# Second projection of block 2 as seven products of quarters, with the order of all steps rewritten from block 1 on

## The chip, the cores and the metric

The kernel runs on one core of one Trainium2 chip. The metric is the device time of one execution in microseconds (us), as a median over runs. The engines are TensorE (PE in the profile; its weight loads are PEld), VectorE (DVE), ScalarE (ACT), GpSimd (POOL) and SyncE (SP), whose queue issues most DMAs.

## What is computed

The reference runs a retention layer over q, k and v (8 sequences, 8 heads, 576 positions, 64 per head) and feeds its output, 4608 tokens of 512, to two projections with a sine between them:

```python
scores = scale * np.matmul(q, k.transpose(0, 1, 3, 2))
Dmat = np.where(rel >= 0, gamma[:, None, None] ** rel, 0.0)      # rel = i - j
x = np.matmul(scores * Dmat, v)        # -> [4608 tokens, 512]
h = x @ w_in                           # 512 -> 2048
s = np.sin(alpha * h)
g = h + s * s / (alpha + 1e-09)
out = g @ w_out                        # 2048 -> 512
```

Inputs and output are float32; the kernel multiplies in float16 and sums in float32.

## The kernel before, in words

**Blocks.** The tokens are nine blocks of 512. Blocks 0 to 7 are the first 512 positions of each sequence; block 8 holds the last 64 positions of all eight (the "last tokens", class `Ends`, whose input tile is `xS`).

**Retention.** For each sequence, q and k are loaded by SP (`load`, L1345 to L1357), scaled and cast to float16 (`cast`, L1396, mostly on GpSimd), and transposed by a DMA on SP's queue (`crossed`, L1418). TensorE then computes outer sums of k and v (`outer`, L1506), scores (`scores`, L1564), values (`values`, L1606) and the part from earlier positions (`add_states`, L1628). All of these are 64x64 matmuls, four of them side by side in the array. VectorE masks the scores (`masked`, L1576), GpSimd carries the state (`more`, L1551 and L1552; `to_state`, L1544), and `keep` copies the result from PSUM to the block's input tile `xT` (L1320 on ScalarE, L1322 on VectorE).

**First projection and sine.** Of each block the 2048 features are 16 chunks of 128. `project` (L1745) is four matmuls of 512 columns into a PSUM bank. `sine` (L1753, ScalarE) reads the bank; `square` is on ScalarE (L1762), VectorE or GpSimd (both L1764); `product` (L1769, VectorE) adds the square, scaled, to the bank's value and writes `gT`. The bank is free after the product. Six banks are passed around (`op`, `h0` to `h2`, `m0`, `m1`), and the retention matmuls and the second projection use the same six.

**Second projection, two ways.** In blocks 0 to 2, `gemm2` (L1785) multiplies directly: 64 matmuls of 512 columns per block, and four `finish` steps copy the result and store it. In blocks 3 to 8 the product of `gT` (2 by 2 quarters) and `w_out` (2 by 2 quarters) is made by Winograd's scheme from seven products of quarters: `part_product` (L1849) is 16 matmuls of 256 columns, so 112 per block. For that VectorE makes eight sums of quarters of `gT` per block (`row_sum`, L1832, each 128x1024, float16, both inputs in SBUF), and once for all blocks eight sums of quarters of `w_out` (`weight_sum`, L1822). `after_product` adds the seven results up: five adds on VectorE (L1880, L1882, L1895) and two copies on ScalarE (L1878, L1893). S3 and T1 are written in place, over `gT` and `w_out`.

**The order.** `TABLE`, a text of some 1,200 lines, lists every step in the order in which it is issued, with its engine (V, A, G), its PSUM bank and the SBUF tile that it takes (`@`). Each engine and queue runs its steps in that order; semaphores do the rest. So the table decides what waits behind what. A line reads, for example:

```
project 2 7 h2
square 2 7 A @ss3
row_sum 3 S3 1 V
part_product 3 1 op
```

The first is chunk 7 of block 2 into bank `h2`; then its square on ScalarE into tile `ss3`; a sum of `gT`'s quarters of block 3 on VectorE; the first of block 3's seven products.

Of the kernel before, what the change touches and what calls it, by code (L numbers as in the profile page):

```python
# [9 lines left out]
F32 = mybir.dt.float32  # L10
F16 = mybir.dt.float16
# [379 lines left out]
gemm2 1 0 h2
product 2 2
gemm2 1 8 h0
gemm2 1 9 h0
gemm2 1 10 h0
sine 2 3 @s1
sine 2 6 @s0
square 2 1 A @ss1
product 2 1
at.scores 3 1 1 m0  # L400
square 2 6 A @ss0
sine 2 0 @s3
square 2 0 A @ss3
at.to_state 3 0 A
product 2 6
at.scores 3 1 0 m1
gemm2 1 11 h0
product 2 0
project 2 4 h1
gemm2 1 1 h2  # L410
sine 2 4 @s2
square 2 4 A @ss2
square 2 3 V @ss1
at.masked 3 1 1 @ret1
project 2 9 m0
gemm2 1 2 h2
product 2 3
product 2 4
project 2 13 h1
gemm2 1 3 h2  # L420
at.masked 3 1 0 @ret3
finish 1 2 V
sine 2 9 @s0
square 2 9 A @ss0
product 2 9
sine 2 13 @s3
finish 1 0
at.scores 3 0 1 m1
at.masked 3 0 1 @ret0
cast 4 k 1 G @k162  # L430
at.outer 4 (0,1) op h0
square 2 13 G @ss3
at.evict_bank 4 0 A @kvs0
at.scores 3 0 0 m0
at.masked 3 0 0 @ret2
project 2 14 h2
at.evict_bank 4 1 V
product 2 13
at.to_state 4 0 A @s160
at.more 4 1 @s321  # L440
project 2 8 op
at.values 3 1 False m1
at.values 3 0 False m0
at.values 3 0 True
at.values 3 1 True
at.add_states 3 0
at.add_states 3 1
sine 2 8 @s2
sine 2 14 @s1
square 2 14 V @ss1  # L450
at.more 4 2 @s320
at.keep 3 0 A V @xT0
at.keep 3 1 A
product 2 14
project 2 10 h0
project 2 11 h1
project 2 12 m0
sine 2 10 @s0
square 2 10 G @ss2
square 2 8 A @ss0  # L460
sine 2 11 @s3
at.to_state 4 1 G
product 2 10
product 2 8
square 2 11 G @ss3
product 2 11
sine 2 12 @s1
project 2 15 m1
sine 2 15 @s0
project 2 5 h2  # L470
sine 2 5 @s2
square 2 5 A @ss1
product 2 5
square 2 15 G @ss2
product 2 15
crossed 4 0 k @kT1
crossed 4 1 q @qT1
load 5 k 1 @raw1
at.more 4 3 @s321
crossed 4 0 q @qT0  # L480
square 2 12 A @ss0
product 2 12
load 5 k 0 @raw4
at.to_state 4 3 G
wait_for_w_out 3
load 5 v 0 @raw0
at.to_state 4 2 A
crossed 4 1 k @kT0
load 5 q 1 @raw2
load 0 v 2  # L490
load 1 v 2
make_mask_halved
project 3 0 h0
sine 3 0 @s3
square 3 0 A @ss2
weight_sum T3 0 V
product 3 0
gemm2 2 0 op
cast 5 v 0 G @v162
cast 5 k 1 G @k160  # L500
load 0 k 2
load 1 k 2
cast 5 q 1 G @q161
project 3 1 h1
sine 3 1 @s2
project 3 2 h2
sine 3 2 @s0
gemm2 2 1 op
project 3 3 m0
sine 3 3 @s1  # L510
square 3 2 A @ss3
load 5 v 1 @raw0
gemm2 2 2 op
gemm2 2 3 op
load 5 q 0 @raw1
project 3 4 m1
cast 5 k 0 G @k163
product 3 2
square 3 3 A @ss2
product 3 3  # L520
finish 2 0
sine 3 4 @s3
square 3 4 A @ss2
project 3 6 h0
sine 3 6 @s3
at.scores 4 0 0 m0
at.masked 4 0 0 @ret3
product 3 4
gemm2 2 4 op
gemm2 2 5 op  # L530
square 3 1 A @ss1
product 3 1
cast 5 v 1 G @v163
square 3 6 A @ss0
gemm2 2 6 op
project 3 7 h1
at.scores 4 1 0 m1
sine 3 7 @s1
product 3 6
cast 0 v 2 G  # L540
at.masked 4 1 0 @ret1
square 3 7 A @ss1
at.scores 4 1 1 m0
at.masked 4 1 1 @ret0
product 3 7
project 3 5 h2
gemm2 2 7 op
sine 3 5 @s3
square 3 5 A @ss2
product 3 5  # L550
project 3 9 h0
weight_sum T2 0 V
load 0 q 2
project 3 10 m0
finish 2 1
project 3 11 h2
# [680 lines left out]
def kernel(  # L1237
# [18 lines left out]
    nc = tc.nc  # L1256
# [772 lines left out]
```

## Time and profile before

| | before |
|---|---|
| runs shown | 297.47 us median (296.52, 297.47, 299.5) |
| profiled execution | 297.29 us |
| its span, first to last instruction | 295.6 us |
| busy: PE, PEld, DVE, ACT, POOL | 96%, 62%, 76%, 74%, 48% |
| granted TensorE clock | 1.00 of full throughout |
| HBM read and written | 36.75 MB, 9.44 MB |

The span leaves out what lies around the first and last instruction, here 1.7 us. Durations in the profile are of single instructions; in a group's row, the busy time is the union, and the mean is over the instructions. A PE instruction's end is modelled, so its length says little: the distance from one start to the next says how fast TensorE works. The profile's chain of waits, followed back from the last instruction, lists merged pieces by their distance in time. In the timeline the pieces of one engine may overlap by the length of the last instruction.

### The profile page before, as it was taken

Reading aid. Unit: us, or ns where it says so; the run is one execution under the profiler, and the core shown is the slowest. Engines: PE = TensorE matmul, PEld = TensorE weight load, DVE = VectorE, ACT = ScalarE, POOL = GpSimd, SP = SyncE. Lnnn points to the kernel's source line nnn. Section 1 sums busy time; section 2 is a strip of 40 time slices with the busy share of each in tenths; the row PEclk is TensorE's granted clock in tenths of the full one; section 3 lists DMA queues with packets and bytes.
Section 4 is the critical chain, followed back from the end, with each engine's and each line's share of the span. In section 5 each row is a group of like instructions: output and inputs, shape, how many; then the busy total and the mean of one; then the engine's idle time right before and its main releaser. Section 6 shows DMA issues by size and latency. Waiting matters only on the chain.

```text
span 295.6 us, 8403 instructions
## 1 busy us (share of the span) xinstructions
PE 284.6 (96%) x3480; PEld 182.2 (62%) x3480; DVE 225.0 (76%) x316; ACT 218.2 (74%) x361; POOL 141.0 (48%) x151
## 2 busy tenths in 40 slices
PE   6799999999999999999999999999999999999993
PEld 4565545555545544456667666666776677676883
DVE  2596979788358677899987898969868785877863
ACT  2578945997695997977878886698689869888500
POOL 5693687664798676636349935756232000000000
PEclk9999999999999999999999999999999999999999
DMA  7999999999997989969899996965323101200124
GB/s 219 347 234 210 253 294 311 262 270 260 226 197 185 163 160 239 226 154 208 156 237 158 256 181 157 243 121 128 87 81 98 38 2 38 73 20 17 57 71 123
DMA packets 121766, 49.95 MB, mean 169 GB/s; under 512 B 78720, under 2 KB 119680, under 8 KB 121728
## 3 DMA queue, kind: packets, MB, share of 16 engines
q1 hardware_dynamic: 118208, 45.04, 63.6%
q0 software_dynamic: 2688, 4.19, 7.8%
q8 instruction: 27, 0.44, 0.7%
q10 hardware_dynamic: 832, 0.18, 0.4%
q14 instruction: 11, 0.09, 0.1%
HBM read 36.75 MB, written 9.44 MB: 156 GB/s over the span
## 4 chain that ended last, share of the span: by engine, by line
PE 85%; DMA 6%; DVE 3%; ACT 2%; POOL 1%; SPq 1%; issue 0%; ACTq 0%; POOLq 0%
PE hps L1745 39%; PE hps L1849 23%; PE ops L1785 14%; DMA w_in<-in_moe_w_in_dram 4%; PE o L1606 3%; PE sc L1564 2%; DMA raw<-in_k_dram 2%; DVE S L1832 1%; PE kv L1506 1%; DVE gT L1769 1%; SPq L1350 1%; PE o L1628 1%; ACT ss L1762 1%; POOL k L1396 1%; ACT s L1753 1%
## 5 line engine op out<-in xcount | busy, mean ns | idle before, releaser
L1769 DVE SCALAR_TENSOR_TENSOR gT<-ss,inva,hps 128x512 f16<-128x512 f16 x144 | 103.5, 743 | 36.4 <-ACT ss L1762 33.1
L1745 PE MATMUL hps<-xT,w_in 128*128 128x512 f16 (+1 forms) x532 | 120.4, 372 | 0.5 <-DMA w_in<-in_moe_w_in_dram 0.4
L1753 ACT ACTIVATE s<-hps,alpha_t 128x512 f16<-128x512 f32 x144 | 96.0, 682 | 31.0 <-PE hps L1745 30.2
L1745 PEld LDWEIGHTS <-w_in 128*128 128x128 f16 x596 | 65.8, 114 | 51.4 <-DMA w_in<-in_moe_w_in_dram 0.9
L1762 ACT ACTIVATE ss<-s 128x512 f16<-128x512 f16 x125 | 76.9, 629 | 6.1 <-DVE gT L1769 3.5
L1785 PE MATMUL ops<-w_out,gT 128*128 128x512 f16 x192 | 46.0, 380 | 0.0
L1849 PEld LDWEIGHTS <-gT 128*128 128x128 f16 x384 | 37.3, 98 | 7.6
L1396 POOL TENSOR_TENSOR k<-raw,cn 128x1024 f16<-128x1024 f32 (+1 forms) x17 | 29.8, 1755 | 17.8 <-DMA raw<-in_k_dram 15.1
L1849 PEld LDWEIGHTS <-S 128*128 128x128 f16 x288 | 28.0, 98 | 6.5 <-DVE S L1832 0.5
L1785 PEld LDWEIGHTS <-gT 128*128 128x128 f16 x192 | 17.8, 98 | 20.4
L1396 POOL TENSOR_TENSOR q<-raw,cn 128x1024 f16<-128x1024 f32 x13 | 25.1, 1937 | 4.3 <-PE o L1606 3.5
L1849 PE MATMUL hps<-w_out,S 128*128 128x256 f16 x192 | 22.9, 273 | 0.2 <-DVE S L1832 0.2
L1849 PE MATMUL hps<-T,gT 128*128 128x256 f16 x192 | 22.8, 273 | 0.0
L1849 PE MATMUL hps<-w_out,gT 128*128 128x256 f16 x192 | 22.8, 273 | 0.0
L1551 POOL TENSOR_TENSOR s<-kvs,cn 128x256 f32<-128x256 f32 x21 | 13.8, 658 | 16.5 <-ACT kvs L1320 8.8
L1322 POOL CAST v<-raw 128x1024 f16<-128x1024 f32 x10 | 10.7, 1074 | 20.6 <-DMA raw<-in_v_dram 17.9
L1576 DVE TENSOR_TENSOR ret<-sc,mask 128x1024 f16<-128x1024 f32 x16 | 19.1, 1219 | 1.6 <-PE sc L1564 1.6
L1832 DVE TENSOR_TENSOR S<-gT,S 128x1024 f16<-128x1024 f16 x24 | 18.7, 786 | 0.1
L1552 POOL TENSOR_TENSOR kvs<-s,kvs 128x256 f32<-128x256 f32 x21 | 16.8, 802 | 3.6 <-DVE kvs L1322 1.2
L1320 ACT CAST xT<-o 128x1024 f16<-128x1024 f32 (+1 forms) x15 | 16.3, 1125 | 2.4 <-PE o L1628 2.2
L1576 DVE TENSOR_TENSOR ret<-sc,mask_halved 128x768 f16<-128x768 f32 x16 | 15.1, 953 | 3.4 <-PE sc L1564 3.2
L1745 PE MATMUL hps<-xS,w_in 128*128 128x512 f16 x64 | 14.8, 379 | 0.0
(78 smaller groups left out, 264.8 us busy)
## 6 DMA issues: line engine op xcount, KB each, us to landing
raw<-in_q_dram SPq DMA_DIRECT2D x16, 512.0 KB, 5.6
out_dram<-osb SPq DMA_DIRECT2D x32, 256.0 KB, 2.3
raw<-in_k_dram SPq DMA_DIRECT2D x8, 512.0 KB, 6.1
raw<-in_v_dram SPq DMA_DIRECT2D x8, 512.0 KB, 6.1
raw<-in_v_dram SPq DMA_DIRECT2D x32, 128.0 KB, 3.6
raw<-in_k_dram SPq DMA_DIRECT2D x32, 128.0 KB, 3.1
w_in<-in_moe_w_in_dram POOLq DMA_DIRECT2D x4, 512.0 KB, 11.7
w_out<-in_moe_w_out_dram POOLq DMA_DIRECT2D x4, 512.0 KB, 12.7
```

Of the source, the lines that this page charges most:

```text
L1320: eng.copy(d_, s_)
L1396: eng.tensor_tensor(dst[:, a0:a1].rearrange("p a r t d -> p t (a r) d"), t_.rearrange("p (t a) x -> p t a x", t=2)[:, :, a0:a1].rearrange( ...
L1551: nc.gpsimd.tensor_tensor(s32, self.kvs[:, c - 1], g1.unsqueeze(2).to_broadcast([P, 4, D]), MULT)
L1552: nc.gpsimd.tensor_tensor(self.kvs[:, c], s32, self.kvs[:, c], ADD)
L1576: nc.vector.tensor_tensor(ret.rearrange("p t (z x) -> p (t z) x", z=2)[:, :, 0:n], sc.rearrange("p t (z x) -> p (t z) x", z=2)[:, :, 0:n], ...
L1745: matmul(hps_of[n, fc][0][:, cols], w_in16[fc // 4][:, a, fc % 4 :: 4], xs[n][:, a, cols], start=(a == 0 and part != 1), stop=(a == KT - 1 ...
L1753: nc.scalar.activation(s_t, hps, mybir.ActivationFunctionType.Sin, bias=0.0, scale=alpha_t[:, fc : fc + 1],)
L1762: nc.scalar.activation(ss_t, s_t, mybir.ActivationFunctionType.Square)
L1769: nc.vector.scalar_tensor_tensor(gT[n][:, fc, :], ss_t, inva[:, fc : fc + 1], hps, MULT, ADD)
L1785: matmul(ops[n, c, cols.start][:, cols], gT[n][:, fk, c * P : (c + 1) * P], w_out16[:, fk, cols], start=(fk == 0), stop=(fk == FC - 1), sk ...
L1832: made = eng.tensor_tensor(out_, x, y, op)
L1849: matmul(acc[:, 256 * j : 256 * j + 256], lhs[:, x, 128 * j : 128 * j + 128], rhs[:, x], start=(tag is not None and j == js[0] and p == 0 ...
```

## The change

1. Block 2's second projection becomes seven products too: its 16 `gemm2` steps and four `finish` steps go, and 8 `row_sum`, 7 `part_product` and 7 `after_product` steps come.
2. The eight `weight_sum` steps, which stood in block 3, stand in block 2, since block 2 now needs them. The tiles T2, T3 and T4 get places of their own; the sums of block 2 lie in tiles that are free then (`early`).
3. The inputs of the last tokens are loaded, cast and transposed at other places, most of them later and spread wider; their tiles share memory with others (`last`), and the tile `xS` is made late.
4. Every step from the end of block 1 on stands in a new order, with other banks and tiles. Engines change too: of the 144 squares 88 are on ScalarE (125 before), 38 on VectorE (11) and 18 on GpSimd (8). Three casts of v go from GpSimd to ScalarE, two casts of last tokens' k and one of their v from GpSimd to VectorE, and some copies from PSUM and state products from ScalarE or GpSimd to VectorE.

The first 349 lines of the table, up to the product of block 1's chunk 15, are as they were.

Core of the diff (line numbers of functions move by 10 to 24: `scores` is L1574, `project` L1757, `square` L1774 to L1776, `product` L1781, `gemm2` L1797, `row_sum` L1856, `part_product` L1873, the adds L1904 to L1919):

```diff
 product 1 15
+make_mask_halved
+crossed 3 0 q @qT2
...
+weight_sum T3 0 V
 gemm2 1 6 h0
+gemm2 1 7 h0
...
-gemm2 2 0 op
+part_product 2 1 op
+square 2 14 G @ss1
...
-square 6 14 A @ss2
+square 6 14 V @ss3
...
+    LAST = {"vs16": "vs16", "qks16": "qks16", "kTs": "raw3", "qTs": "raw5"}
+    def last(name, shape, dtype):
+        if name not in of_last:
+            of_last[name] = work.tile(shape, dtype, tag=LAST[name], bufs=1, name=name)
+        return of_last[name]
...
+    EARLY = {("S1", 1): ("vs16", 0), ("S4", 0): ("vs16", 1), ("S4", 1): ("qks16", None)}
...
+    def piece(name, p, n=None):
+        if name[0] == "T":
+            if name not in pieces:
+                pieces[name] = work.tile([P, 2, 4, 256], F16, tag=name, bufs=1, name=name)
+            return pieces[name][:, p]
+        early = n < 3
...
-        tag = {"low": "qT1", "mid": "u2"}[name]
+        tag = {"low": "qT1" if n > 2 else "xS", "mid": "u2"}[name]
```

Three places show how the order moves. The first is TensorE at sequence 3's scores of its second half, between block 1's second projection (`gT_1035` there) and block 2's first. `sc` is a bank of scores, `ops` one of the second projection, `hps` one of the first; "..." stands for rows that repeat. Before:

```order
L1785 MATMUL ops_1633<-w_out16_74,gT_1035 128x512
L1785 LDWEIGHTS gT_1035
...
L1564 LDWEIGHTS kT2_622
L1564 MATMUL sc_1650<-qT3_502,kT2_622 64x128
...
L1564 MATMUL sc_1675<-qT3_502,kT2_622 64x128
...
L1745 LDWEIGHTS w_in16_1_71
L1745 MATMUL hps_1697<-xT2_1547,w_in16_1_71 128x512
```

and now:

```order
L1757 MATMUL hps_1641<-xT2_1545,w_in16_0_70 128x512
L1574 LDWEIGHTS kT2_620
L1574 MATMUL sc_1648<-qT3_500,kT2_620 64x128
...
L1797 LDWEIGHTS gT_1033
L1797 MATMUL ops_1610<-w_out16_74,gT_1033 128x512
...
L1574 LDWEIGHTS kT2_620
L1574 MATMUL sc_1680<-qT3_500,kT2_620 64x128
...
L1757 LDWEIGHTS w_in16_1_71
L1757 MATMUL hps_1705<-xT2_1545,w_in16_1_71 128x512
```

The two groups of 16 score matmuls stood next to each other; now a part of the second projection stands between them. Counted over all of TensorE's order, retention matmuls stood in 39 stretches between other matmuls, and now stand in 46.

The second place is VectorE between blocks 6 and 7 (`ss` is a square, `S_0` and `S_1` are sums of quarters, `mid` and `low` partial results). Before:

```order
L1832 TENSOR_TENSOR gT<-gT 128x4x256
L1832 TENSOR_TENSOR S_0_2493<-gT 128x1024
L1769 SCALAR_TENSOR_TENSOR gT<-ss_541,inva,hps 128x512
L1832 TENSOR_TENSOR S_0_2495<-gT,S_0_2493 128x1024
L1769 SCALAR_TENSOR_TENSOR gT<-ss_543,inva,hps 128x512
L1769 SCALAR_TENSOR_TENSOR gT<-ss_565,inva,hps 128x512
```

and now:

```order
L1856 TENSOR_TENSOR gT<-gT 128x4x256
L1776 TENSOR_TENSOR ss_525<-s_517 128x512
L1686 TENSOR_TENSOR rets<-scs,mask 128x1024
L1781 SCALAR_TENSOR_TENSOR gT<-ss_525,inva,hps 128x512
L1776 TENSOR_TENSOR ss_563<-s_550 128x512
L1781 SCALAR_TENSOR_TENSOR gT<-ss_563,inva,hps 128x512
L1856 TENSOR_TENSOR S_0_2521<-gT 128x1024
```

VectorE's queue now holds squares (L1776) right ahead of the products that use them.

The third place is the end of GpSimd's queue. Before:

```order
L1551 TENSOR_TENSOR s_625<-kvs_248,cn 128x256
L1552 TENSOR_TENSOR kvs_248<-s_625,kvs_248 128x256
L1380 TENSOR_TENSOR qs_4074<-qs_3907,cn 128x2x4x64
L1380 TENSOR_TENSOR qs_4135<-qs_3916,cn 128x2x4x64
L1322 CAST vs_4137<-vs_3781 128x512
L1544 TENSOR_TENSOR sS<-kvs_248,cn 128x256
```

and now:

```order
L1390 TENSOR_TENSOR qks_3102<-qs_3893,cn 128x2x4x64
L1776 TENSOR_TENSOR ss_541<-s_523 128x512
L1323 CAST vs_2642<-vs_3899 128x512
L1776 TENSOR_TENSOR ss_525<-s_517 128x512
L1554 TENSOR_TENSOR sS<-kvs_246,cn 128x256
L1776 TENSOR_TENSOR ss_539<-s_523 128x512
L1776 TENSOR_TENSOR ss_539<-s_517 128x512
L1776 TENSOR_TENSOR ss_541<-s_550 128x512
```

GpSimd's queue ended with block 7's last state before; now squares of blocks 6 to 8 follow to the end.

More of the change, by code (lines that the diff above doesn't have):

```diff
@@ L975 @@
[L975 to L1001 removed]
+project 5 12 h1
@@ new lines @@
+product 7 1
+sine 7 3 @s2
+row_sum 6 S1 0 V
+square 7 3 A @ss1
+project 7 5 m1
+product 7 3
+ends.keep 0 0 V
+project 7 8 h0
+ends.keep 0 1 A
+project 7 7 h1
+sine 7 5 @s1
+square 7 5 V @ss0
+product 7 5
+project 7 9 h2
+project 7 11 m0
+after_product 6 6
+part_product 6 7 - first=6
+sine 7 7 @s2
+square 7 7 A @ss1
+load 7 v 2
+product 7 7
+cast 6 v 2 V
+sine 7 8 @s2
+square 7 8 V @ss3
+product 7 8
+at.to_state 7 3 G
+sine 7 9 @s2
+sine 7 11 @s1
+square 7 9 V @ss3
+product 7 9
+after_product 6 7
```

1574 lines of the change are left out of this document (773 added, 801 removed).

## The prediction

> **What bounds the kernel now.** I read the chain of waits first, then busy time by stretches, then the distances between starts on TensorE. The chain says that four fifths of the end are TensorE's:
>
> ```profile
> PE 284.6 (96%) x3480; PEld 182.2 (62%) x3480; DVE 225.0 (76%) x316; ACT 218.2 (74%) x361; POOL 141.0 (48%) x151
> ...
> PE 85%; DMA 6%; DVE 3%; ACT 2%; POOL 1%; SPq 1%; issue 0%; ACTq 0%; POOLq 0%
> 118.81 3.45 PE hps L1745 x16
> 84.77 3.45 PE ops L1785 x16
> 136.11 1.75 PE hps L1849 x16
> ```
>
> The first row is the busy time of the engines; the last three are pieces of the chain (start, length, what). They give the pace: a matmul of 512 columns takes 3.45/16 = 0.2156 us in either projection, one of 256 columns 1.75/16 = 0.1094 us. Now the changed part: the new order begins after the first products of block 1's second projection, at 74.3 us, and TensorE's last matmul ends near 291.1 us. By stretches (start:end, length, then the busy us of PE, PEld, DVE, ACT, POOL):
>
> ```profile
> 74.30:100.00 25.70, 25.61 (x320) 13.30 (x320) 15.35 (x20) 19.56 (x40) 20.80 (x20) 1.00 0.91 195
> 100.00:130.00 30.00, 30.00 (x340) 15.35 (x339) 22.87 (x30) 25.72 (x45) 19.10 (x22) 1.00 0.95 200
> 130.00:160.00 30.00, 30.00 (x376) 19.60 (x378) 26.51 (x35) 24.38 (x39) 16.49 (x17) 1.00 0.86 189
> 160.00:190.00 30.00, 29.60 (x279) 19.85 (x267) 26.90 (x35) 23.67 (x39) 20.45 (x19) 1.00 0.98 203
> 190.00:220.00 30.00, 30.00 (x451) 20.68 (x453) 23.77 (x35) 23.93 (x38) 12.72 (x14) 1.00 0.49 113
> 220.00:250.00 30.00, 29.91 (x412) 20.46 (x401) 22.84 (x33) 25.11 (x41) 3.71 (x4) 1.00 0.15 46
> 250.00:275.00 25.00, 25.00 (x170) 17.33 (x168) 18.94 (x29) 20.67 (x34) 0.00 (x0) 1.00 0.10 33
> 275.00:291.10 16.10, 16.06 (x146) 14.05 (x144) 12.00 (x20) 3.52 (x6) 0.00 (x0) 1.00 0.25 76
> sum 216.80, PE 216.16 PEld 140.63 DVE 169.19 ACT 166.54 POOL 93.28; mean PE 27.02 PEld 17.58 DVE 21.15 ACT 20.82 POOL 11.66
> ```
>
> The last row sums 74.3 to 291.1 us. TensorE misses 0.64 of 216.8 us, at full clock (the 1.00 behind POOL). So time is what TensorE has to do, plus these 0.64, and a transfer or another engine counts only when it makes TensorE wait. VectorE is at 169.2/216.8 = 78%, and at 26.90/30 = 90% in its densest stretch, the one where TensorE loses most (0.40).
>
> **What TensorE saves.** Block 2's 64 direct matmuls cost 64 x 0.2156 = 13.80 us; the 112 of seven products 112 x 0.1094 = 12.25 us. That is **-1.55 us**, all on the path. The first projection and the retention keep their matmuls, number for number.
>
> **What the new order adds on TensorE.** Retention matmuls (64x64) now stand in 46 stretches instead of 39. What a stretch costs beyond its own work is seen where the same work stands in groups of 16 and of 32 (TensorE's timeline: start, length; read the distances of starts):
>
> ```profile
> 110.74 1.89 PE L1745 MATMUL hps<-xT,w_in 128*128 128x512 f16 x8
> 112.56 0.37 PE L1564 MATMUL sc<-qT,kT 64*64 64x128 f16 x16
> 112.86 2.76 PE L1785 MATMUL ops<-w_out,gT 128*128 128x512 f16 x12
> 115.46 1.03 PE L1745 MATMUL hps<-xT,w_in 128*128 128x512 f16 x4
> 116.41 0.54 PE L1564 MATMUL sc<-qT,kT 64*64 64x128 f16 x32
> 116.89 1.05 PE L1745 MATMUL hps<-xT,w_in 128*128 128x512 f16 x4
> ```
>
> From 110.74 to 112.86 are 2.12 us; take off eight matmuls at 0.2156 (1.72) and a stretch of 16 costs 0.40. From 115.46 to 116.89 are 1.43 us; less four (0.86), a stretch of 32 costs 0.57. Two of 16 are 0.80, so every split costs about 0.80 - 0.57 = 0.23 us. Seven more stretches are 7 x 0.23 = **+1.6 us**. No wait is in it, so nothing hides it. The two terms cancel: -1.55 + 1.6 = +0.05 us. This is the step that I trust most, and it leaves the sign to the waits.
>
> **What VectorE gets.** Durations by rows (busy us, mean ns, or min/median/max ns):
>
> ```profile
> L1764 DVE TENSOR_TENSOR ss<-s x11: 417/419/994, 23.8 to 99.2; 128x512 f16<-128x512 f16 x11
> L1832 DVE TENSOR_TENSOR S<-gT,S x24: 681/684/2073, 132.3 to 284.8; 128x1024 f16<-128x1024 f16 x24
> L1895 DVE TENSOR_TENSOR osb<-hps,low 128x512 f32<-128x512 f32 x13 | 8.9, 685 | 2.9 <-PE hps L1849 2.7
> L1322 DVE CAST xT<-o 128x1024 f16<-128x1024 f32 x1 | 1.3, 1343 | 0.7 <-PE o L1628 0.7
> L1322 DVE CAST xT<-o 128x512 f16<-128x512 f32 x5 | 3.6, 733 | 0.5 <-ACT xT L1320 0.5
> L1396 DVE TENSOR_TENSOR q<-raw,cn 128x512 f16<-128x512 f32 x2 | 1.3, 688 | 1.0 <-DMA raw<-in_q_dram 1.0
> L1544 DVE TENSOR_TENSOR s<-kvs,cn 128x256 f16<-128x256 f32 x1 | 0.4, 424 | 0.0
> ```
>
> 27 squares at 0.42 are 11.3 us; eight sums of quarters at 0.69 are 5.5; five adds of products at 0.69 are 3.4. The moved copies and casts: two of `xT` 2.7, three of `xS` at 0.73 2.2, two casts of last tokens' k at 0.69 1.4, four state products 1.7, one cast of v 0.4, less a copy of `kvs` that goes to ScalarE, 0.7: 7.7. Together 27.9 us. The eight sums of `w_out` only move, to 15 to 40 us of TensorE work earlier.
>
> The maxima in the first two rows are the other half. The trace shows what makes them, on VectorE, GpSimd and TensorE:
>
> ```profile
> 169.41 1.91 POOL L1396 TENSOR_TENSOR q<-raw,cn 128x1024 f16<-128x1024 f32 x1 [0.20 <-DMA raw<-in_q_dram]
> 169.44 2.42 DVE L1832 TENSOR_TENSOR S<-gT 128x1024 f16<-128x1024 f16 x1
> ...
> 180.94 1.90 POOL L1396 TENSOR_TENSOR k<-raw,cn 128x1024 f16<-128x1024 f32 x1 [4.79 <-DMA raw<-in_k_dram]
> 181.32 2.07 DVE L1832 TENSOR_TENSOR S<-gT,S 128x1024 f16<-128x1024 f16 x1
> 183.45 1.26 PE L1849 MATMUL hps<-w_out,S 128*128 128x256 f16 x10 [0.19 <-DVE S L1832]
> ```
>
> A sum of 0.68 us that starts while GpSimd works on a cast ends only 0.5 us or more after the cast, and in the second case TensorE waits for it. Behind a held-up sum or square VectorE's queue holds the products, which free the banks for the next chunks: that is how a hold-up reaches TensorE. The groups give the bill so far:
>
> ```profile
> L1832 DVE TENSOR_TENSOR S<-gT,S 128x1024 f16<-128x1024 f16 x24 | 18.7, 786 | 0.1
> L1832 DVE TENSOR_TENSOR S<-gT 128x1024 f16<-128x1024 f16 x12 | 10.6, 880 | 0.4 <-issue 0.2
> L1832 DVE TENSOR_TENSOR gT<-gT 128x1024 f16<-128x1024 f16 x12 | 10.1, 847 | 0.0
> L1764 DVE TENSOR_TENSOR ss<-s 128x512 f16<-128x512 f16 x11 | 5.1, 473 | 2.8 <-ACT s L1753 2.8
> L1764 POOL TENSOR_TENSOR ss<-s x8: 1039/1040/1042, 28.1 to 104.5; 128x512 f16<-128x512 f16 x8
> ```
>
> 48 sums took 39.4 us instead of 48 x 0.684 = 32.8, 11 squares 5.1 instead of 4.6: 7.1 us too much over 59, 0.12 each. The change brings 35 more such operations (4.2 us), and ten more squares of 1.04 us on GpSimd (last row), most of them where its queue was empty (POOL 3.71 and 0.00 in the stretches from 220 us). The Trainium skill (SBUF — State Buffer, Who interferes with whom) has the rule for it: a VectorE instruction with two SBUF inputs and a GpSimd instruction that reads SBUF exclude each other, and the later one waits for the whole of the first. The two collisions above agree; by the rule, with GpSimd busy 43% (93.28 of 216.8) and half of its mean 0.91 us left (93.28 us over the 102 instructions of the eight rows), 35 operations would wait 6.9 us, an estimate from that page's rule and these rows.
>
> VectorE so comes to 169.2 + 27.9 + 4.2 = 201.3 us in a stretch of 216.8: **93%**, over the 90% at which TensorE began to lose. Below: at 88% (130 to 160 us) TensorE lost nothing. Above: 0.40 per 30 us throughout makes 7.2 x 0.40 = 2.9 us. I take the middle, 1.45, less the 0.64 that are there already: **+0.8 us**.
>
> **What costs nothing.** ScalarE loses 37 squares; it is at 166.5 of 216.8 and not what TensorE waits for. SP's count of stores is the same (four of 256 KB). The last tokens' loads move to where the DMA engines are half idle (0.49, then 0.15 in the rows from 190 us); sequence 6's first loads stand some 30 to 60 us of TensorE work earlier, behind nothing urgent. SP's wait for `w_out`, now late, holds a queue that has only stores left. The start, to 74.3 us, is untouched, and the tail still ends in two half-size adds and a store.
>
> **Sum.** 297.29 - 1.55 + 1.6 + 0.8 = 298.1 us, 0.2% over the median of the runs shown: no change that a measurement tells, which is about 1% here.
>
> **The rivals.**
>
> *A, VectorE sets the pace (slower).* If it can't get beyond some 91%, because each square still waits for its sine and each product for its square, the stretch becomes 201.3/0.91 = 221.2 us, 4.4 longer than 216.8: 297.3 + 0.05 + 4.4 = 301.7 us. It decides from 93% down. For it: in six of eight stretches VectorE is under 80% although TensorE is full. Against it: a square on VectorE takes 0.42 us and no hop to ScalarE, so its waits shrink. The Trainium skill (Perfetto Trace Analysis, Identifying the Most-Contended Engine) would have it so already: it judges TensorE by weight loads (here 140.6 of 216.8, 65%) and VectorE by busy time (78%). The distances of starts say otherwise for before.
>
> *B, the saving comes through (faster).* If the 0.64 us of waits vanish and the extra stretches fall into waits that would be there anyway, time is 297.29 - 1.55 - 0.64 = 295.1 us; with the splits paid 296.7. For it: the order is free to use VectorE's shorter squares. Against: the split's cost is TensorE's own time.
>
> *C, a late transpose in sequence 7.* Between the cast of its second half's q on GpSimd and the scores that need it stand now two chunks and one product, 2 x 0.86 + 1.75 = 3.5 us. The cast takes 1.9 us (rows at 169.41 and 180.94) and the transpose lands 3.6 us after its issue (median):
>
> ```profile
> DMA to landing us min/median/max: 2.9/3.6/6.4
> ```
>
> That is 5.5 us, so TensorE waits up to 2.0 us if the cast starts no sooner than its place: 298.1 + 2.0 = 300.1. Against: GpSimd may reach it early.
>
> **Chances.** My forecast 0.50, A 0.22, B 0.16, C 0.12. Faster by over 1% (under 294.5) is only B's lower end, 0.06; slower by over 1% (over 300.4) is most of A and a little of C, 0.22; within 1% the rest, 0.72. The range reaches from B's end, 295.1, to just over A's price, 302.0.
>
> **What would show it.** Right: TensorE's distances unchanged at 0.2156 and 0.1094; some 46 stretches of 64x64 matmuls; VectorE near 257 us busy in all (225.0 before); TensorE's missing time in the changed part between 1 and 2 us; last matmul near 291.5. Wrong, if splits cost less than 0.1 us each (then near 297), if sums and squares run undisturbed, or if TensorE waits for `gT` or `ss` by over 3 us (then A). A wait of scores for `qT` near 210 us would be C.

## The result, and the profile after

The changed kernel takes **308.29 us** (median of 4 runs, 306.12 to 309.25), the kernel before, run beside it, 298.49 us: a ratio of 1.0325, with an interval of 1.024 to 1.041. Ratios are worked out from undisturbed runs alone, so they can differ a little from the ratio of the medians given. The forecast was 298.1 us and no change. The profiled execution took 308.37 us with a span of 306.7 us, 11.1 us more than before.

First the busy time of the engines, the granted clock in 40 slices, and the chain of waits, of the changed kernel:

```profile
PE 286.9 (94%) x3528; PEld 187.5 (61%) x3528; DVE 245.7 (80%) x367; ACT 198.2 (65%) x321; POOL 142.0 (46%) x151
...
PEclk9599999999997999999999999999999999999998
...
PE 66%; DMA 18%; SPq 5%; ACT 4%; POOL 3%; DVE 2%; issue 2%; POOLq 0%; ACTq 0%
```

TensorE's share of the chain fell from 85% to 66%, and DMA and SP's queue rose from 7% to 23%. VectorE got the work it was to get, but it isn't in the chain. The slice of 92 to 100 us has a granted clock of 0.7.

By stretches, from the last steps that both kernels share on (start:end, length, then busy us of PE, PEld, DVE, ACT, POOL, clock, DMA):

```profile
76.80:100.00 23.20, 19.31 (x219) 9.57 (x209) 11.69 (x16) 13.66 (x27) 17.79 (x21) 0.93 0.94 205
100.00:130.00 30.00, 28.75 (x378) 17.65 (x376) 27.10 (x37) 23.57 (x39) 16.63 (x14) 1.00 0.93 193
...
160.00:190.00 30.00, 30.00 (x370) 20.82 (x369) 27.23 (x41) 22.08 (x35) 16.90 (x17) 1.00 1.07 185
...
250.00:275.00 25.00, 24.16 (x249) 16.60 (x249) 23.29 (x38) 15.70 (x25) 4.16 (x4) 1.00 0.11 35
...
sum 226.20, PE 219.01 PEld 146.67 DVE 190.18 ACT 146.56 POOL 94.33; mean PE 27.38 PEld 18.33 DVE 23.77 ACT 18.32 POOL 11.79
```

TensorE misses 7.2 of 226.2 us (0.64 before), more than half of it in the first row. In the row from 160 us, where VectorE is 91% busy (27.23 of 30 us), it misses nothing; in that from 250 us, at 93% (23.29 of 25), it misses 0.84 us, which is one wait for `mid`, a partial result. What TensorE waited for (us in all, times, longest), and where:

```profile
PE sc L1574 <- DMA qT<-q: 3.7, 1, 3.7
...
PE hps L1757 <- DVE gT L1781: 1.0, 1, 1.0
...
PE hps L1873 <- DVE mid L1904: 0.9, 1, 0.9
```

```profile
93.56 0.64 PE L1574 MATMUL sc<-qT,kT 64*64 64x128 f16 x16 [3.72 <-DMA qT<-q]
94.13 3.90 PE L1797 MATMUL ops<-w_out,gT 128*128 128x512 f16 x12
97.97 0.42 PE L1574 MATMUL sc<-qT,kT 64*64 64x128 f16 x16
```

The scores of sequence 3's second half wait 3.72 us for its q, and then 12 matmuls take 97.97 - 94.13 = 3.84 us instead of 12 x 0.2156 = 2.59: 1.25 us more, since 5 of them start at about twice the usual distance (0.1 us of it is the step to the next scores, which f1 below pays too). That wait and its aftermath are some 4.9 us.

Another part of the loss lies ahead of everything that was reordered. The last step that both orders share, the product of chunk 15 of block 1, begins at 74.0 us before and at 77.7 us after. The steps up to it are the same, one by one. What differs is how long the loads take. The page's DMA issues (count, KB each, median us to landing), before:

```profile
raw<-in_k_dram SPq DMA_DIRECT2D x8, 512.0 KB, 6.1
...
raw<-in_v_dram SPq DMA_DIRECT2D x32, 128.0 KB, 3.6
raw<-in_k_dram SPq DMA_DIRECT2D x32, 128.0 KB, 3.1
```

and after:

```profile
raw<-in_k_dram SPq DMA_DIRECT2D x8, 512.0 KB, 7.2
...
raw<-in_v_dram SPq DMA_DIRECT2D x32, 128.0 KB, 4.5
raw<-in_k_dram SPq DMA_DIRECT2D x32, 128.0 KB, 5.0
```

Same transfers, 1 to 2 us longer each. The clue is a line of the diff that the account of the change above left out, since it looks like nothing:

```diff
-        first = work.tile([P, 1], F32, tag="first", bufs=1, name="first")
+        first = inva[:, 0:1]
```

`first` is a scratch tile of 4 bytes per partition that a first sine warms up on; it took 32 bytes of SBUF (the memory that all tiles lie in). Without it, every tile that is allocated behind it (all that q, k and v are loaded, cast and transposed into, and more) moves down by 32 bytes: from multiples of 512 to 32 bytes below them (`raw0` from 60416 to 56288, with other tiles gone ahead of it).

### The profile page after: what moved, and what is told of

It reads as the page before. It is cut to its first block, busy times and chain, and to the rows that moved or that the text cites. A ratio compares the mean times of both kernels' runs of the same rounds, so it can differ in the third digit from the quotient of the medians.

```text
span 306.7 us, 8526 instructions
## 1 busy us (share of the span) xinstructions
PE 286.9 (94%) x3528; PEld 187.5 (61%) x3528; DVE 245.7 (80%) x367; ACT 198.2 (65%) x321; POOL 142.0 (46%) x151
## 4 chain that ended last, share of the span: by engine, by line
PE 66%; DMA 18%; SPq 5%; ACT 4%; POOL 3%; DVE 2%; issue 2%; POOLq 0%; ACTq 0%
PE hps L1757 30%; PE hps L1873 27%; DMA raw<-in_v_dram 6%; DMA w_in<-in_moe_w_in_dram 4%; DMA raw<-in_k_dram 4%; PE ops L1797 4%; PE sc L1574 2%; DMA out_dram<-osb 2%; DMA qT<-q 2%; SPq L1360 2%; POOL k L1406 1%; ACT s L1765 1%; PE o L1616 1%; SPq L1355 1%; PE kv L1516 1%
## 5 line engine op out<-in xcount | busy, mean ns | idle before, releaser
L1757 PE MATMUL hps<-xT,w_in 128*128 128x512 f16 (+1 forms) x532 | 121.4, 372 | 2.2 <-DVE gT L1781 1.0
L1781 DVE SCALAR_TENSOR_TENSOR gT<-ss,inva,hps 128x512 f16<-128x512 f16 x144 | 103.9, 742 | 16.3 <-ACT ss L1774 14.1
L1757 PEld LDWEIGHTS <-w_in 128*128 128x128 f16 x596 | 65.3, 115 | 51.6 <-issue 2.6
L1774 ACT ACTIVATE ss<-s 128x512 f16<-128x512 f16 x88 | 55.2, 629 | 7.3 <-DVE gT L1781 5.1
L1776 POOL TENSOR_TENSOR ss<-s 128x512 f16<-128x512 f16 x18 | 19.3, 1077 | 75.2 <-ACT s L1765 62.3
L1873 PEld LDWEIGHTS <-gT 128*128 128x128 f16 x448 | 43.5, 98 | 9.7 <-issue 1.2
L1797 PE MATMUL ops<-w_out,gT 128*128 128x512 f16 x128 | 31.6, 390 | 0.0
L1873 PEld LDWEIGHTS <-S 128*128 128x128 f16 x288 | 27.9, 98 | 5.7
L1873 PE MATMUL hps<-T,gT 128*128 128x256 f16 x224 | 26.6, 273 | 0.9 <-DVE mid L1904 0.9
L1406 POOL TENSOR_TENSOR q<-raw,cn 128x1024 f16<-128x1024 f32 x13 | 26.2, 2019 | 2.6 <-DMA qT<-q 1.4
L1873 PE MATMUL hps<-w_out,gT 128*128 128x256 f16 x224 | 26.6, 273 | 0.0
L1776 DVE TENSOR_TENSOR ss<-s 128x512 f16<-128x512 f16 x38 | 19.7, 520 | 6.8 <-ACT s L1765 6.2
L1873 PE MATMUL hps<-w_out,S 128*128 128x256 f16 x192 | 22.8, 273 | 0.0
L1797 PEld LDWEIGHTS <-gT 128*128 128x128 f16 x128 | 12.0, 100 | 14.2 <-issue 1.7
L1321 ACT CAST xT<-o 128x1024 f16<-128x1024 f32 (+1 forms) x13 | 14.0, 1097 | 6.0 <-PE o L1638 6.0
L1856 DVE TENSOR_TENSOR S<-gT,S 128x1024 f16<-128x1024 f16 x24 | 16.6, 713 | 0.1
L1574 PEld LDWEIGHTS <-kT 64*64 64x64 f16 x512 | 8.2, 112 | 12.3 <-issue 10.0
```

What stands on the lines that cost most here:

```text
L1406: eng.tensor_tensor(dst[:, a0:a1].rearrange("p a r t d -> p t (a r) d"), t_.rearrange("p (t a) x -> p t a x", t=2)[:, :, a0:a1].rearrange( ...
L1574: matmul(sc[halves(g), t, c : c + n], kT[halves(t), 2 * a + r, halves(g)], qT[halves(t), 2 * a : 2 * a + 2, 64 * g + i0 : 64 * g + 64], st ...
L1757: matmul(hps_of[n, fc][0][:, cols], w_in16[fc // 4][:, a, fc % 4 :: 4], xs[n][:, a, cols], start=(a == 0 and part != 1), stop=(a == KT - 1 ...
L1774: nc.scalar.activation(ss_t, s_t, mybir.ActivationFunctionType.Square)
L1776: eng.tensor_tensor(ss_t, s_t, s_t, MULT)
L1781: nc.vector.scalar_tensor_tensor(gT[n][:, fc, :], ss_t, inva[:, fc : fc + 1], hps, MULT, ADD)
```

## The experiments

Two theories for the first part: **places** (the loads are slower because their targets lie off) against **order** (they are slower since the DMA engines do other work at those times). For the rest: **late steps** (a few waits that the new order makes), against **price** (the seven products cost more than they save, on VectorE or in extra stretches).

### Both kernels once more

*c_before*, nothing changed. 

> The kernel before, unchanged, for a profile beside the other kernels of this call. The first product of block 1's last chunk (the last instruction that both orders share on VectorE) starts at 74.0 us in the first profile of before and at 77.7 us in that of the change, with the same instructions ahead of it. If that difference of 3.7 us comes with the chip's DMA of the day, this profile should show it near 76 to 78 us; if the change causes it, near 74 us.

*c_after*, nothing changed. 

> The change, unchanged, on the chip of the other three. Theory: 7 to 8 us of its extra time lie behind the shared part: 3.7 us in which TensorE waits for the transposed q of sequence 3, 1.2 us of half clock behind that wait, 1.2 us near 114 us, 1.1 us near 249 us. Rival (VectorE sets the pace): the loss is spread over all stretches behind 100 us. Both expect about 308 us; the first expects the same four gaps at the same places.

Measured: 298.62 us, ratio 0.9995 (0.9966 to 1.0024), and 309.09 us, ratio 1.0343 (1.0298 to 1.0388). So the loss belongs to the change and not to the day. The wait of the scores is there again, 3.39 us, with 7 matmuls at half speed behind it (1.47 us).

### Two ways to move the late scores

*e1_scores_later*: scores of sequence 3's second half behind two more chunks, side by side.

```diff
-at.scores 3 1 0 m1
...
-at.scores 3 1 1 m1
...
+at.scores 3 1 0 m1
+at.scores 3 1 1 m0
...
 project 2 8 op
...
+gemm2 1 0 h1
 project 2 9 m1
...
-gemm2 1 0 h1
 sine 2 9 @s1
```

> The change with sequence 3's two groups of second-half scores moved behind chunks 7 and 4 of block 2 and side by side, some 4.3 us of TensorE work later (the last part of block 1's second projection that starts is moved one place up). Theory (late transpose, then half clock): the 3.7 us wait and the slow matmuls behind it go, 4 to 5 us less than the change, a ratio near 1.015 to the kernel before. Rival (VectorE sets the pace): no more than 0.5 us less, since VectorE's work is the same; the time would show up as later waits for products.

Measured: 305.7 us, ratio 1.0233 (1.0186 to 1.028). TensorE's order around them now reads:

```profile
94.64 0.64 PE L1574 MATMUL sc<-qT,kT 64*64 64x128 f16 x32
...
98.15 1.02 PE L1757 MATMUL hps<-xT,w_in 128*128 128x512 f16 x4 [1.02 <-DVE ret L1586]
99.74 0.42 PE L1574 MATMUL sc<-qT,kT 64*64 64x128 f16 x16 [0.57 <-DMA qT<-q]
...
114.15 1.02 PE L1757 MATMUL hps<-xT,w_in 128*128 128x512 f16 x4 [1.74 <-DVE gT L1781]
```

The wait is gone, a third of the loss with it, and waits of 1.02, 0.57 and 1.74 us stand further on.

*e2_transpose_first*: the transpositions of that half, and a cast, ahead of two loads.

```diff
+cast 3 q 1 G @q161
 at.more 3 1 @s320
...
+crossed 3 1 k @kT2
+crossed 3 1 q @qT3
 load 4 k 0 @raw4
...
-crossed 3 1 k @kT2
...
-cast 3 q 1 G @q161
...
-crossed 3 1 q @qT3
```

> The change with only the queues altered: GpSimd casts the second half of sequence 3's q ahead of the state sums, and SP issues the two transposes that the scores need ahead of sequence 4's loads. TensorE's and VectorE's orders are those of the change. Theory: the transposes land some 5 us sooner, the wait of 3.7 us and the half clock go, 4 to 5 us less than the change; sequence 4's loads come some 3 us later and hit nothing. Rival (DMA bandwidth, not the place in the queue): the transpose still lands after 90 us and the time stays within 1 us of the change.

Measured: 308.58 us, ratio 1.034 (1.03 to 1.0381): no gain. The first half's q, loaded and transposed behind all that, is late now:

```profile
96.55 1.03 PE L1797 MATMUL ops<-w_out,gT 128*128 128x512 f16 x4
101.92 0.32 PE L1574 MATMUL sc<-qT,kT 64*64 64x128 f16 x4 [4.35 <-DMA qT<-q]
```

Moving one transfer ahead made another late here.

### The tiles' places

*e3_after_on_512*: the changed kernel with its tiles back on multiples of 512. The tile `first` is restored; for its room the tile `zero`, which feeds idle matmuls ahead of the changed part, is halved and the idle matmuls doubled.

```diff
-        first = inva[:, 0:1]
+        first = work.tile([P, 1], F32, tag="first", bufs=1, name="first")
...
-    zero = work.tile([P, 512], F16, tag="zero", bufs=1, name="zero")
+    zero = work.tile([P, 256], F16, tag="zero", bufs=1, name="zero")
```

> The change with its table untouched, and its working tiles put back on multiples of 512 bytes: the 4-byte tile called first is made again, and the tile of zeros for the idle matmuls is halved to make room (7 idle matmuls of 256 columns and 1 more stand for 4 of 512: same work). In before every working tile starts at a multiple of 512; in the change that small tile is gone and every one starts 32 bytes below a multiple. Packets of 512 bytes took 27 ns in before and 34 ns in the change between 5 and 15 us. Theory (the places of the tiles slow the DMAs): packets back to 27 to 28 ns, the last shared product back from 77.6 to about 74.6 us, the wait for sequence 3's transposed q under 1 us, and 298 to 300 us in all. Rival (the order alone loses the time, the 3 us in the shared part come from elsewhere): no more than 1 us less than the change's 309.

*b1_before_off_512*: the kernel before with nothing but the line on `first` changed, so that its tiles lie 32 bytes below multiples of 512.

```diff
-        first = work.tile([P, 1], F32, tag="first", bufs=1, name="first")
+        first = inva[:, 0:1]
```

> The kernel before with its own table and one line of the change: the 4-byte tile called first is taken away (the first column of inva is used), so that every working tile starts 32 bytes below a multiple of 512. Theory (places of the tiles): packets of 512 bytes 32 to 34 ns, the last shared product 3 us later at 77.6 us, and 302 to 306 us in all, with no other change. Rival (the order alone): 298.5 us, as before.

*b2_before_256_off*: the kernel before with `first` of 288 bytes, so that its tiles lie on odd multiples of 256.

```diff
-        first = work.tile([P, 1], F32, tag="first", bufs=1, name="first")
+        first = work.tile([P, 72], F32, tag="first", bufs=1, name="first")[:, 0:1]
```

> The kernel before with that small tile made larger (288 bytes), so that every working tile starts 256 bytes behind a multiple of 512. It tells how far a tile has to be aligned. If multiples of 256 are enough: 298.5 us and 27 to 28 ns for a packet of 512 bytes, as before. If it has to be 512: about what the kernel off by 32 bytes takes.

Measured, with the mean time of a DMA packet of 512 bytes (from the trace, in two stretches of the span) and the start of the last shared product:

| kernel | tiles start at | packet, 5 to 15 us | 30 to 60 us | last shared product | ratio to before |
|---|---|---|---|---|---|
| before (c_before) | 512 x n | 27.0 ns | 27.5 ns | 74.6 us | 0.9995 (0.9966 to 1.0024) |
| before (b2) | 512 x n + 256 | 27.1 | 27.5 | 74.3 | 1.0006 (0.9977 to 1.0035) |
| before (b1) | 512 x n - 32 | 34.1 | 31.7 | 77.6 | 1.0254 (1.0184 to 1.0325) |
| after (c_after) | 512 x n - 32 | 34.1 | 31.5 | 77.6 | 1.0343 (1.0298 to 1.0388) |
| after (e3) | 512 x n | 27.0 | 27.6 | 74.1 | 1.0155 (1.0094 to 1.0217) |

Places it is: the old order with the new places is 2.5% slower, the new order with the old places loses 1.9% less (1.0343/1.0155 = 1.0185). The engines' own work is not slower in b1: a sine takes 682 ns on average and a product 742, against 682 and 743 before. But its loads land about as late as the changed kernel's, and its scores wait:

```profile
raw<-in_v_dram SPq DMA_DIRECT2D x32, 128.0 KB, 4.5
raw<-in_k_dram SPq DMA_DIRECT2D x32, 128.0 KB, 4.1
```

```profile
93.30 0.64 PE L1564 MATMUL sc<-qT,kT 64*64 64x128 f16 x32 [1.51 <-DMA qT<-q]
```

b2 says that multiples of 256 are enough. The Trainium skill (DMA: Bandwidth & Descriptors, How a descriptor splits into AXI transactions) has a rule of this kind: a transfer is cut at multiples of 256 bytes, and a piece that starts off them pays for the bytes ahead of it too. The Trainium skill tells this of what is read, and here it is the written side that lies off. The trace agrees in the direction; by the beats that this page of the Trainium skill gives a packet of 512 bytes at 32 below would take 23 instead of 16, 1.44 times as long (an estimate from its rule), and 34/27 = 1.26 is measured.

### What is left in the new order

On multiples of 512 the changed kernel still loses 1.55% (302.38 us, where the theory of places had said 298 to 300). In e3 the scores wait too, if less:

```profile
88.30 0.42 PE L1574 MATMUL sc<-qT,kT 64*64 64x128 f16 x16 [2.17 <-DMA qT<-q]
88.65 4.33 PE L1797 MATMUL ops<-w_out,gT 128*128 128x512 f16 x12
```

The scores start there 14.2 us behind the last shared product (88.3 - 74.1); in the kernel before they began 14.1 us behind it (88.15 - 74.0), and in c_before 14.6, after a wait of 0.43 us for the same q. The new order asks for them at 86.1 us, 2 us sooner, and the transfer comes no sooner.

*e4_on_512_scores_later*: e3 with e1's move. 

> The change with its tiles on multiples of 512 and, besides, sequence 3's second-half scores later and side by side, as in the run before. If the wait for the transpose was only a consequence of slow DMAs, this gives no more than 0.5 us over the kernel with the tiles on 512 alone, by one stretch of 64x64 matmuls less (0.2 us). If that wait is a fault of the order by itself, it gives 3 to 5 us more.

Measured: 301.9 us, ratio 1.0151 (1.0109 to 1.0192), the same as e3. By the number alone the wait would have been a consequence of the slow loads, but e3's trace has it at 2.17 us without them. Again the wait goes and others come (0.70, 0.90 and 1.97 us).

*f1_queue*: e3, with two steps swapped instead.

```diff
+cast 3 q 1 G @q161
 cast 4 q 1 G @q160
-cast 3 q 1 G @q161
...
+crossed 3 1 q @qT3
 cast 4 k 0 G (0) @k160
 wait_for_w_in 3
 load 4 q 0 @raw2
-crossed 3 1 q @qT3
```

> The changed kernel with its tiles on multiples of 512 bytes (302.4 us measured), and two steps swapped: the cast of sequence 3's second-half q stands ahead of that of sequence 4's q on GpSimd, and its transposition is issued two places earlier on SP, ahead of the gate on w_in and of the load of sequence 4's q. Theory O (the rest of the loss is waits that the new order makes): the scores no longer wait 2.3 us near 86 us, TensorE's clock is not halved behind that wait, and nothing else moves: 302.4 - 1.8 - 1.3 = 299.3 us, ratio 1.004. Rival M (each wait that is removed comes back at the next late step, as in the two earlier attempts): 301.5 to 302.5, ratio 1.011 to 1.015.

Measured: 300.25 us, ratio **1.0067** (1.0045 to 1.009):

```profile
87.59 0.42 PE L1574 MATMUL sc<-qT,kT 64*64 64x128 f16 x16 [0.40 <-DMA qT<-q]
87.94 2.76 PE L1797 MATMUL ops<-w_out,gT 128*128 128x512 f16 x12
```

0.40 us of waiting instead of 2.17, and the 12 matmuls in 2.76 us instead of 4.33. This edit overtakes a gate (a step that holds SP's queue until `w_in` is loaded), a load and one cast, nothing that is needed soon. The time lies between the two theories: most of the gain stays, and its trace has two waits that e3's has not, of 0.59 us near 96 us and of 1.32 us near 131 us.

*f2_sums*: e3, with VectorE's queue changed only: the second halves of T3 and T2 beside the first, T1 0 and S4 0 behind the products that they held up, and `after_product 6 6` ahead of `ends.keep 0 0 V`.

> The changed kernel on multiples of 512 bytes with only VectorE's queue changed: the second halves of the weight sums T3 and T2 are made beside the first halves, in stretches where VectorE is idle; T1's and the row sum S4's first halves stand behind the products that they held up; the add of product 6 of block 6 stands ahead of the last tokens' copy. Theory O: the waits of 1.3 us near 110 us, of about 1.0 us near 245 us vanish, and the wait near 86 us stays: 302.4 - 2.2 = 300.2 us, ratio 1.007. Rival M: waits come back elsewhere, 302 us, ratio 1.013.

Measured: 304.17 us, ratio 1.0186 (1.0154 to 1.0217): no gain, by the midpoints a loss. What the new order of the sums did stands on VectorE, GpSimd and TensorE:

```profile
115.89 2.30 DVE L1856 TENSOR_TENSOR early_S<-gT 128x1024 f16<-128x1024 f16 x1
```

```profile
115.74 6.07 POOL L1406 TENSOR_TENSOR k<-raw,cn 128x1024 f16<-128x1024 f32 x3
```

```profile
118.90 1.02 PE L1757 MATMUL hps<-xT,w_in 128*128 128x512 f16 x4 [1.82 <-DVE gT L1781]
```

This row sum, S2's second half, was not moved itself. In e3 it ran ahead of the three casts on GpSimd and took 0.68 us; now it begins beside them, takes 2.30 us, and the product behind it in VectorE's queue makes TensorE wait 1.82 us. Waits of 1.10 us near 122 us and of 0.60 near 83 are new too, and so is a pause of 1.14 us near 106 us, which g1 below comes back to. The wait near 245 us did go, and so did the one near 86 us, but for 0.54 us, though it was to stay.

*f3_queue_sums*: f1 and f2 together. 

> Both edits together, on multiples of 512 bytes. Theory O: 302.4 - 3.1 - 2.2 = 297.1 us, ratio 0.996, and TensorE's missing time from 74 us on under 3 us. Rival M: 300 us or more, ratio 1.006 or more.

Measured: 302.14 us, ratio 1.0127 (1.0089 to 1.0164). The swap gains beside f2, the sums lose beside f1, and the time is in the range of rival M.

*f4_block2_direct*: e3, with block 2's second projection direct as it was (its direct matmuls read a quarter of `w_out` that T1 has replaced by then; only its time is meant).

```diff
-part_product 2 1 op
+gemm2 2 0 op
+gemm2 2 1 op
...
-after_product 2 2
+finish 2 0
...
-row_sum 2 S1 1 V
```

> The changed kernel on multiples of 512 bytes, but block 2's second projection is made directly (64 matmuls of 512 columns at the places of the seven products; no row sums and no adds of products for block 2; the weight sums stay where they are). All other steps keep the new order. By the sum of the prediction the seven products save 1.55 us of TensorE; their row sums and adds take 8 x 0.69 + 2 x 0.69 us of VectorE. Theory P (the products are worth what TensorE saves, and the loss is the order's): 302.4 + 1.5 = 303.9 us, ratio 1.020. Rival V (the products' row sums on VectorE cost TensorE more than the products save): 301 us or less, ratio 1.011 or less.

Measured: 307.5 us, ratio 1.0311 (1.0276 to 1.0347), more than either theory said, and not by the matmuls alone: a wait took over. TensorE's retention waits for GpSimd, and GpSimd for a load:

```profile
134.22 0.53 PE L1614 MATMUL o<-ret,v 64*64 64x128 f16 x16 [3.13 <-POOLq L1468]
```

```profile
134.14 1.04 POOL L1321 CAST v<-raw 128x1024 f16<-128x1024 f32 x1 [9.12 <-DMA raw<-in_v_dram]
```

The retention's signal is relayed through GpSimd's queue, behind the cast of sequence 5's v, which waits for its load. f1 has the same wait at that place (1.3 us), so it is one of the new order's late steps.

*f5_two_waits*: f1, with two steps moved.

```diff
-cast 5 v 1 G @v162
...
 at.values 4 0 False m0 relay=G
+cast 5 v 1 G @v162
...
+after_product 6 6
 ends.keep 0 0 V
```

> The changed kernel on multiples of 512 bytes with the earlier transposition (300.25 us measured), and two more steps moved: the cast of sequence 5's second-half v stands behind the relay of sequence 4's retention on GpSimd instead of ahead of it, and the add of product 6 of block 6 ahead of the last tokens' copy on VectorE. Theory O (what is left is waits of the order): the waits of 1.5 us near 131 us and 1.1 us near 245 us vanish: 300.25 - 2.6 = 297.7 us, ratio 0.998. Rival M (waits come back at the next late step): 299.5 to 300.5 us, ratio 1.004 to 1.007.

Measured: 299.56 us, ratio **1.0029** (1.0001 to 1.0057). Its waits from 74 us on, and its two densest stretches for VectorE:

```profile
PE hps L1757 <- DVE gT L1781: 2.0, 1, 2.0
PE o L1616 <- DVE ret L1586: 0.3, 1, 0.3
PE hps L1757 <- DVE xT L1323: 0.2, 1, 0.2
```

```profile
160.00:190.00 30.00, 29.72 (x350) 20.89 (x349) 27.96 (x42) 20.49 (x33) 17.73 (x18) 1.00 0.62 139
...
250.00:275.00 25.00, 25.00 (x214) 17.44 (x213) 23.28 (x39) 14.07 (x23) 6.85 (x6) 1.00 0.13 44
```

Both waits are gone. The one of 2.0 us, near 106 us, is the packed sums ahead of chunk 11's product: the last of them, for T2, runs beside a cast on GpSimd and takes 2.40 us. It was 1.16 us in e3, and so the time is in the range of rival M.

*f6_weight_sums_early*: f5, with the second halves of T3 and T2 out of that pack.

```diff
+weight_sum T3 0 V
+weight_sum T3 1 V
 at.keep 2 1 A V
...
 weight_sum T2 0 V
+weight_sum T2 1 V
...
-weight_sum T3 1 V
...
-weight_sum T2 1 V
```

> As f5, and the second halves of the weight sums T3 and T2 stand beside the first halves, where VectorE is idle, instead of ahead of the products of chunks 11 and 10 of block 2. T1's and S4's first halves stay. Theory O: up to 0.7 us of waits near 108 us fewer than f5: 297.0 us, ratio 0.996. Rival L (sums that are moved fall upon other casts of GpSimd and are held up there, as in f2): 298.5 us or more, ratio 1.001 or more.

Measured: 299.57 us, ratio 1.0048 (1.0021 to 1.0074): nothing that can be told from f5, as rival L said. The wait of 2.0 us is gone in its trace, but two others stand there. The sums moved ahead run beside casts at 82.5 us, two in 2.21 us, and TensorE waits 0.71 us for the product behind them. And near 106 us it pauses for nothing that the profile shows:

```profile
106.98 2.32 PE L1757 MATMUL hps<-xT,w_in 128*128 128x512 f16 x10 [1.11 <-issue]
```

*f7_direct_without_waits*: f5, with block 2 direct as in f4. 

> As f5, but block 2's second projection is made directly, as in f4: 64 matmuls of 512 columns at the places of the seven products, no row sums and no adds for block 2, the weight sums where they were (so the direct matmuls read a quarter of w_out that T1 has replaced by then: the time alone is meant). Theory P (the seven products are worth what TensorE saves, 1.55 us): f5 + 1.5 us, 299.2 us if f5 comes out at 297.7. Rival V (their row sums and adds on VectorE cost as much as they save): the same as f5 or less.

Measured: 300.66 us, ratio 1.0092 (1.0064 to 1.0121), clear of f5's interval. Its waits of the same stretch:

```profile
PE sc L1572 <- DVE gT L1779: 0.6, 1, 0.6
PE o L1614 <- DVE ret L1584: 0.4, 1, 0.4
PE sc L1572 <- DMA qT<-q: 0.2, 1, 0.2
PE hps L1755 <- DVE xT L1321: 0.2, 1, 0.2
PE hps L1755 <- DVE gT L1779: 0.2, 1, 0.2
```

Its span is 298.9 us, less 1.6 of waits 297.3; f5's is 298.1, less 2.5 is 295.6. So the seven products save 1.7 us in the traces; by the ratios it is 0.6% or 1.9 us, by the medians 1.1 us. That is theory P, with a size that is known to about 1 us.

*g1_fill_wait*: e3 with `keep_busy 16 h2` ahead of the late scores, which gives TensorE something to do in the wait. 

> The changed kernel on multiples of 512 bytes (302.4 us measured), with 16 idle matmuls of 256 columns (16 x 0.109 = 1.75 us) put into TensorE's queue ahead of the late scores of sequence 3, and nothing else changed: the transposition lands as late as before. Theory H (the clock drops because TensorE stands idle for over some 2.2 us): the matmuls behind the scores run at 0.216 us, 302.4 - 1.3 = 301.1 us, ratio 1.011. Rival (the matmuls are slow there for another reason, or the idle matmuls only take longer themselves): six of about 0.43 us again, 302.4 us or more, ratio 1.015.

Measured: 307.17 us, ratio 1.0326 (1.028 to 1.0371), though the place itself did as theory H said:

```profile
86.39 1.91 PE L1931 MATMUL idle<-zero 128*128 128x256 f16 x16 [0.49 <-DVE gT L1782]
88.23 0.42 PE L1575 MATMUL sc<-qT,kT 64*64 64x128 f16 x16
88.58 2.76 PE L1798 MATMUL ops<-w_out,gT 128*128 128x512 f16 x12
...
107.39 0.30 PE L1639 MATMUL o<-qT,s 64*64 64x128 f16 x1 [3.86 <-issue]
```

The scores start where they did in e3 (88.23 and 88.30 us), and the 12 matmuls behind them take 2.76 us instead of 4.33, so it was the idleness that halved their speed in e3. But 15 us on TensorE stands still for 3.86 us in the middle of a group, for nothing that the profile shows, and 7 matmuls of half speed follow (1.46 us). In the trace the next block of TensorE's instructions, 16 KB, is fetched at 105.0 us, 1.5 us into that pause and 15.1 us after the block before it. There are 27 such fetches, one for some 130 matmuls. The other kernels bear out that the pause is a wait for it: f2, f4, f6 and c_after have a pause without a cause in the profile too, of 1.14, 1.40, 1.11 and 0.67 us. In each it stands ahead of TensorE's 1,371st matmul (the 1,372nd in g1), whatever that matmul works on, and ends 2.3 to 2.8 us after the start of a fetch. In g1 the 16 added matmuls let TensorE reach that number while it is still at the 64x64 matmuls, of which it had started some 128 in the 2 us before. No run changed the fetch alone.

## Why the prediction was wrong

**The step that failed** is "The start, to 74.3 us, is untouched", and with it "what costs nothing" for SP and the loads. No step of the start was changed, but the place of its tiles was, and 3.0 to 3.7 us were lost ahead of the first new step (77.6 against 74.6 us in c_after and c_before, 77.7 against 74.0 in the first pair). In all this is 1.9 of the 3.4% (c_after to e3). The profile of before could not show it; the diff could have raised the question, since a tile vanished ahead of all others.

**Late scores.** Rival C had the mechanism, a transposition that lands too late for scores, and put it at sequence 7; it was at sequence 3, at the first of the three places that the account of the change shows. The new split was priced there as a stretch of 0.23 us, and not asked when its q lands. On multiples of 512 this wait and its half-speed matmuls are 0.9% (e3 to f1). Two smaller late steps are another 0.4% by the middle of the ratios (f1 to f5), whose intervals overlap; 0.3% is left.

**What TensorE saves**, -1.55 us: right. 1.7 us in the traces, f7 to f5.

**What the new order adds on TensorE**, +1.6 us: right in kind, too large in size. The stretches are 46, as counted. Read from the starts of the matmuls around each, less the waits, those behind 74.5 us cost 19.2 us in before (25 of them) and 20.1 in f5 (32): 0.9 us for seven more, 0.13 each instead of 0.23. Whole spans say more. f7 has block 2's old matmuls in the new order, and without its waits is 297.3 us long; before, without the 0.4 us of waits over 0.1 us that its trace has from 74 us on, 295.2: 2.1 us, of which 1.2 are not accounted for (c_before gives 295.9 instead of 295.2, so that single spans are good to about 1 us). The net of both terms, forecast at +0.05, is 295.6 - 295.2 = +0.4 us in f5. So the sum, 298.1 us, was that of a kernel whose tiles stay in place and whose transfers are in time, and f5, the nearest to that, has 1.0029. That it comes so near the forecast is luck in part: its waits are 2.5 us instead of 1.45, its stretches cheaper.

**VectorE**, +0.8 us, and rival A. The waits for VectorE behind 76 us are 2.1 us (1.0, 0.9 and 0.2), where the prediction had 1.45, so the size was near; rival A's sign, over 3 us, did not show. But the step that led to it, more work and so a busy share beyond 90%, is wrong on both counts. VectorE's groups after (busy us, mean ns):

```profile
L1776 DVE TENSOR_TENSOR ss<-s 128x512 f16<-128x512 f16 x38 | 19.7, 520 | 6.8 <-ACT s L1765 6.2
...
L1856 DVE TENSOR_TENSOR S<-gT,S 128x1024 f16<-128x1024 f16 x24 | 16.6, 713 | 0.1
...
L1856 DVE TENSOR_TENSOR gT<-gT 128x1024 f16<-128x1024 f16 x14 | 10.9, 776 | 0.0
...
L1856 DVE TENSOR_TENSOR S<-gT 128x1024 f16<-128x1024 f16 x12 | 8.4, 709 | 0.3 <-issue 0.2
```

First the work. All 56 sums of quarters took 40.2 us (the rows above and 4.3 us in rows named `early_`), where 48 took 39.4 before, and 38 squares took 19.7. Over what they take alone, 0.684 and 0.419 us, that is 5.7 us of hold-ups for 94 operations, against 7.1 for 59 before; the prediction had 11.3. VectorE's busy time rose by 20.7 us instead of 32.1. (Where the prediction counts 102 instructions of GpSimd, for an estimate outside its sum, the eight rows have 96.)

Then the threshold. It rested on one row of before, whose 0.40 us are single waits. In the changed kernel TensorE misses nothing at 91% and 0.84 us at 93%; in f5 it misses 0.28 of 30 us in one row at 93% and nothing in another. The 0.84 us went with one add that was moved ahead of one copy. A busy share decides nothing by itself; f2 shows what does: one sum in the wrong place beside GpSimd costs 1.8 us.

**Rival B** (the saving comes through) was not near either: the changed kernel is 3.25% slower, and f5, with its late steps mended, still has a lower bound of 1.0001.

## What to carry to other kernels

When a change adds, drops or resizes a tile, print the start addresses of all tiles of before and after, and keep the targets of DMAs on multiples of 256 bytes: 32 bytes in front of the other tiles cost more here (1.9 to 2.5%) than the seven products save (0.6%). When an order is rewritten, check for each first use of a transferred tile how long after its issue it stands now, and move a late transfer past steps that nobody needs soon, not past the next one that is as late. Here a loss that consisted of several waits was paid back only where they were removed one by one, each looked at in the new trace.

## What had not been expected of the hardware

- A packet of 512 bytes whose target starts 32 bytes below a multiple of 256 takes 34 ns instead of 27 in the first loads (5 to 15 us), 32 instead of 27.5 from 30 to 60 us; the medians of the 128 KB loads are 4.1 to 5.1 us in b1, after and c_after, and 3.1 to 3.7 in before, c_before, b2 and e3.
- After a pause of 2.33 us or more, TensorE ran its next 5 to 7 recorded matmuls of 512 columns at half speed, 1.0 to 1.5 us in all (pauses of 2.33, 3.31, 3.55, 3.88, 4.05 and 4.51 us in e3, f4, c_after, after, g1 and e2); after pauses of up to 2.15 us it did not (f5; 2.13 in e4, 2.02 in f3). A pause is here the distance of two starts less the pace of the matmul ahead, up to 0.2 us more than in the profile's brackets. In each of the six traces the granted clock is then 0.50 for one stretch of 3.41 us. In e3 (the clock is the figure behind POOL):

```profile
86.28:89.68 3.40, 1.38 (x21) 0.79 (x22) 1.21 (x2) 2.26 (x4) 3.07 (x2) 1.00 1.01 213
89.70:93.09 3.39, 3.39 (x16) 1.08 (x18) 1.60 (x3) 0.70 (x2) 3.17 (x6) 0.50 1.10 148
```

The Trainium skill (TensorE: Matmul & The Clock Gate, What's actually happening) lets the clock drop after an idle window of about 3.4 us. The length of the stretch agrees; but here TensorE was busy for 1.38 us of the 3.40 ahead of it, so the window need not be idle throughout, and the measurement decides. Whether the length of a pause counts or how it falls on such stretches was not tried.
- Sixteen matmuls put into an empty place cost 5 us further on (g1), where TensorE stood still for 3.86 us around a fetch of its instructions; four other traces have pauses of 0.67 to 1.40 us at the same place in its count of matmuls.
